# A planned kernel on one core: the same units in another written order, with other cells, other banks and 45 fill matmuls for 33

## The chip, the cores and the metric

The kernel runs on one core of one Trainium2 chip. The metric is device time in microseconds (us) of one execution. Three runs of the kernel before gave 459.48, 458.48 and 455.35 us, a median of 458.48 us.

## The reference

Inputs are float32: queries, keys and values of 4 batches, 8 heads, 768 positions and 40 channels, and three gates. Three blocks follow each other.

1. A recurrent attention over the 768 positions: a running maximum of the gates gives a forget and an input factor per position; a 40x40 state `C` and a vector `n` are updated with them, and each position reads `o * (C q) / max(|n q|, 1)`.
2. A gated convolution on the 320 joined channels: `(sigmoid(causal 5-tap conv of x) * (x @ w_val)) @ w_out`.
3. A mixer: the real part of a two-dimensional FFT over positions and channels is added to `x` (this is `u`), `u` is normalised, and `u + max(un @ w_ch1, 0) @ w_ch2` with 1280 hidden channels is returned.

## The kernel before

Per batch the 768 positions are six chunks of 128. A chunk (`a_fb` to `a_tr`) spreads the gates with a small matmul, scans them on VectorE into decays `d`, forms scores, state updates and outputs with many small matmuls on quarters of the array, divides, and transposes. After three chunks a half batch goes through the convolution (`p_conv`: 1 activation and 4 multiply-adds on VectorE per 128 channels; for three of the pieces five matmuls), the two products (`p_val`, `p_z`) and a fold; after six, the FFT as cosine and sine matmuls (`b_s`, `b_d`), the normalisation (`b_ln`), transposes (`b_ut`) and the feed-forward block (`m_1`, `m_2`) in three row blocks of five slices.

Matrix operands are split in two float32r parts, so that a product is three or four passes. The weights come as 64-bit words and are turned into float32 on the chip: `to_f32` takes two VectorE instructions that read two SBUF operands (`mk<-raw,mk`) and two that read one (`mk<-mk`) for each piece of 640 columns, and GpSimd forms the low parts. All of this conversion stands in batch 0.

**The order is written out.** The functions only record; each call becomes a unit (one VectorE, ScalarE, GpSimd or DMA instruction, or one group of matmuls), numbered as recorded. `emit` goes through `ORDER` and issues the units; each engine runs its own units in that order, and semaphores for true dependences come from the framework. `CELL` gives each working tile its SBUF slot or its first PSUM bank, which decides whose readers it must wait for. `FILLS` puts extra matmuls of ones on ones ahead of a unit, into a bank that is given as the third number; the second is how many. All DMAs but one are issued by SyncE (SP).

Units that the text names (batch, then chunk or block, in brackets):

| unit | engine | what |
|---|---|---|
| 11, 12, 13 | SP | loads of the forget gates `gf`, the input gates `gi`, the identity `pat` |
| 150 | SP | load of 64 rows of `w_val`, 160 KB |
| 25 | PE | first transposes of `gi` |
| 24, 26, 70 | DVE | scan to `eg`, copy to `isT`, first scan to `d` |
| 152, 153 | DVE | `mk<-mk` of a weight tail |
| 68, 78 | PE | gate spread of chunks (0,0) and (0,1) |
| 267 | PE | `a_pv` (0,3): reads `cc` and `e1`, then scores, then `d` |
| 266, 285, 288 | DVE | last `cc` of (0,3); scan to `d` of (0,5); product into `e1` for (0,5) |
| 416, 232 | PE | `a_pv` (0,5); the second `val` group (0,0,1) |
| 490, 516 | PE | the one-row matmul of `b_d` (0,0); first transposes of normalised rows |
| 690 | PE | scores and state products of chunk (1,0) |
| 514, 515, 576 | DVE, DVE, PE | low parts of the transposed rows (0,0); the first feed-forward group that reads them |
| 581, 583, 579, 580, 695 | PE, DVE, PE, PE, PE | `m_1` (0,0,1), its `hl`, the two halves of `m_2` (0,0,0), `a_pv` (1,0) |
| 788, 789, 813 | PE, DVE, PE | `val` (1,0,2), the product that reads it, `a_pv` (1,3) |

Of the kernel before, what the change touches and what calls it, by code (L numbers as in the profile page):

```python
# [176 lines left out]
]  # L177
FILLS = [
    (25, 15, 1), (72, 4, 1), (87, 2, 6), (485, 4, 6), (489, 3, 6), (516, 2, 6), (576, 3, 6),
]  # L180


# [1062 lines left out]
```

## Time and profile before

| | before |
|---|---|
| median of three runs | 458.48 us (455.35 to 459.48) |
| profiled execution, its own time | 456.86 us |
| span of that execution | 454.7 us |
| TensorE (PE) matmul busy | 436.1 us, 96% |
| VectorE (DVE) busy | 334.5 us, 74% |
| ScalarE (ACT) busy | 174.4 us, 38% |
| GpSimd (POOL) busy | 161.6 us, 36% |
| mean granted TensorE clock | 0.992 |

All rows are of the one profiled execution; its time outside the span is 2.2 us. Almost all instructions carry the line of the loop in `emit` (L304; L360 are fills and L367 is the warm-up), so the rows are read by tile names: `bank<-xH,wvH` is a matmul of a `val` group, `hl` the low part of a hidden slice. PE is the matmul row, PEld the weight loads, SPq the queue of DMA issues. Matmul ends are modelled, so starts are the safer reading.

### The profile page before, as it was taken

The page shows a single profiled execution, that of the slowest core. Times are in us where ns is not written, and L with a number is a line of the kernel's source. Part 1 is how long each engine was busy: PE and PEld are TensorE (multiplying, and loading weights), DVE is VectorE, ACT ScalarE, POOL GpSimd, SP SyncE. Part 2 cuts the span into 40 slices and gives each one's busy share as a digit, 9 for nine tenths or more (in the row PEclk, how much of TensorE's full clock was granted, in tenths as well). Part 3 has the DMA queues.
Part 4 walks back from the last instruction along what each step waited for, and adds up shares of the span by engine and source line. Part 5 has one row for each costly group of instructions (what it writes and reads, how often), then busy time and mean ns, then how long its engine had stood idle before and what let it go on. Part 6 is the DMA issues. An engine that isn't in the chain of part 4 may idle for free. (4 is left out here: it accounts for less than half of the span.)

```text
span 454.7 us, 13773 instructions
## 1 busy us (share of the span) xinstructions
PE 436.1 (96%) x5734; PEld 410.5 (90%) x5734; DVE 334.5 (74%) x810; ACT 174.4 (38%) x412; POOL 161.6 (36%) x210
## 2 busy tenths in 40 slices
PE   9978898799999999999999999999999999999996
PEld 8866777598999999999999999999999998999996
DVE  7999799989998886596686967788766846642421
ACT  4544644363343633232442524214425323160310
POOL 5666147577664513043524114544031130010000
PEclk9999899989999999999999999999999999999999
DMA  7779757661144511020303410213020000000011
GB/s 207 224 209 257 208 178 248 184 195 32 60 126 141 158 55 64 2 78 29 112 16 94 141 45 0 68 39 88 4 88 1 2 0 16 16 1 0 16 45 58
DMA packets 23301, 39.83 MB, mean 88 GB/s; under 512 B 4753, under 2 KB 14289, under 8 KB 23241
## 3 DMA queue, kind: packets, MB, share of 16 engines
q1 hardware_dynamic: 23192, 38.90, 28.7%
q8 instruction: 45, 0.74, 0.7%
q14 instruction: 16, 0.12, 0.1%
q0 software_dynamic: 48, 0.07, 0.1%
HBM read 32.77 MB, written 4.23 MB: 81 GB/s over the span
## 5 line engine op out<-in xcount | busy, mean ns | idle before, releaser
L304 PE MATMUL bank<-uu,w1H 128*128 128x256 f32 x480 | 92.5, 285 | 0.7 <-DVE uu L304 0.6
L304 PEld LDWEIGHTS bank<-uu,w1H 128*128 128x128 f32 x480 | 74.4, 188 | 2.9 <-issue 1.6
L304 PE MATMUL bank<-w2H,hh 128*128 128x320 f32 x240 | 75.9, 324 | 0.1
L304 PE MATMUL bank<-w2L,hh 128*128 128x320 f32 x240 | 72.4, 309 | 0.0
L304 PE MATMUL bank<-uu,w1L 128*128 128x256 f32 x240 | 67.3, 280 | 0.0
L304 ACT ACTIVATE hh<-bank 128x512 fp32r<-128x512 f32 x60 | 34.9, 594 | 69.7 <-PE bank L304 61.0
L304 DVE SCALAR_TENSOR_TENSOR hl<-bank,hh 128x512 fp32r<-128x512 f32 x60 | 40.4, 683 | 21.5 <-ACT hh L304 21.2
L304 PE MATMUL bank<-w2H,hl 128*128 128x320 f32 x240 | 54.9, 310 | 0.0
L304 DVE SCALAR_TENSOR_TENSOR bank<-xT,cw,bank 128x384 f32<-128x384 f32 x84 | 50.0, 617 | 2.1 <-ACT bank L304 1.3
L304 PEld LDWEIGHTS bank<-w2H,hh 128*128 128x128 f32 x240 | 45.1, 188 | 0.9 <-ACT dg L304 0.4
L304 PEld LDWEIGHTS bank<-w2L,hh 128*128 128x128 f32 x240 | 45.2, 188 | 0.2
L304 PEld LDWEIGHTS bank<-uu,w1L 128*128 128x128 f32 x240 | 45.3, 189 | 0.0
L304 PEld LDWEIGHTS bank<-w2H,hl 128*128 128x128 f32 x240 | 40.2, 188 | 0.0
L304 POOL TENSOR_TENSOR cc<-cc,fcol 128x164 f32<-128x164 f32 x40 | 19.9, 498 | 52.6 <-DVE cc L304 32.8
L304 DVE TENSOR_TENSOR z<-z,bank 128x320 f32<-128x320 f32 (+2 forms) x76 | 26.4, 375 | 16.3 <-PE bank L304 15.0
L304 POOL TENSOR_TENSOR gL<-gg,gH 128x384 fp32r<-128x384 f32 x16 | 18.5, 1158 | 54.1 <-ACT gH L304 40.4
L304 PE MATMUL bank<-uu,w1U 128*128 128x256 f32 x120 | 33.7, 281 | 0.0
L304 PE MATMUL bank<-uu,w1T 128*128 128x256 f32 x120 | 33.7, 281 | 0.0
L304 POOL TENSOR_TENSOR kvo<-kvo,r 128x320 f32<-128x320 f32 x24 | 17.8, 743 | 39.8 <-DVE r L304 32.7
L304 DVE TENSOR_TENSOR_SCAN d<-bank,pat 128x512 f32<-128x512 f32 x24 | 29.0, 1214 | 2.6 <-PE bank L304 2.4
L304 DVE SCALAR_TENSOR_TENSOR mk<-raw,mk 128x640 int32<-128x640 int32 (+2 forms) x30 | 27.2, 918 | 0.1
L304 POOL TENSOR_TENSOR e<-e,qk 128x512 f32<-128x512 f32 (+1 forms) x18 | 22.9, 1273 | 9.9 <-DMA qk<-in_qk_dram 5.4
(153 smaller groups left out, 998.8 us busy)
## 6 DMA issues: line engine op xcount, KB each, us to landing
kvo<-in_kvo_dram SPq DMA_DIRECT2D x24, 484.0 KB
qk<-in_qk_dram SPq DMA_DIRECT2D x48, 160.0 KB
raw<-in_w_dram SPq DMA_DIRECT2D x9, 640.0 KB
out_dram<-z SPq DMA_DIRECT2D x24, 160.0 KB
e<-sce SPq DMA_DIRECT2D x30, 80.0 KB
cs<-in_c_cs_dram SPq DMA_DIRECT2D x2, 386.0 KB
raw<-in_w_dram SPq DMA_DIRECT2D x4, 160.0 KB
raw<-in_w_val_dram SPq DMA_DIRECT2D x1, 640.0 KB
```

The lines of the kernel that those rows point to most:

```text
L304: i = getattr(engine, method)(*a, **k)
```

## The change

`ORDER`, `CELL` and `FILLS` are replaced; nothing else is. The units are the same 1996 and none is added. By engine, of 375 matmul groups 231 keep their place in PE's own order within two places (the farthest moves 25), of 809 VectorE units 343 do (44), of 410 ScalarE units 182 (184), of 206 GpSimd units 149 (34), of 196 DMA issues 79 (28). It comes from a search whose judgement of an order also counts stretches in which TensorE is little busy.

The diff, cut to the lines that the text speaks of (each `ORDER` line is whole):

```diff
 ORDER = [
-    11, 6, 12, 7, 16, 4, 0, 1, 13, 149, 150, 2, 15, 17, 9, 18, 22, 23, 32, 19, 21, 20, 14, 316, 33, 34, 115, 151,
-    114, 5, 315, 35, 25, 152, 139, 26, 24, 68, 153, 70, 8, 29, 116, 59, 117, 56, 72, 36, 30, 58, 154, 39, 140, 57,
...
-    280, 214, 47, 137, 127, 215, 283, 260, 287, 144, 158, 258, 217, 189, 266, 170, 216, 364, 159, 267, 145, 269,
-    285, 191, 218, 307, 220, 226, 136, 291, 171, 219, 270, 268, 236, 256, 161, 221, 271, 261, 272, 227, 288, 290,
...
-    713, 510, 523, 694, 516, 512, 525, 363, 397, 517, 518, 680, 735, 684, 513, 355, 681, 519, 1115, 708, 515, 514,
-    576, 526, 528, 577, 686, 685, 406, 530, 798, 687, 529, 531, 678, 719, 549, 710, 391, 578, 392, 826, 393, 532,
-    398, 581, 582, 583, 715, 533, 394, 808, 579, 580, 695, 534, 720, 712, 407, 600, 585, 535, 709, 697, 395, 696,
...
+    2, 7, 4, 11, 6, 150, 12, 13, 8, 3, 16, 15, 139, 1, 0, 17, 9, 22, 18, 114, 5, 32, 117, 23, 19, 115, 14, 25, 21,
+    20, 33, 37, 149, 58, 57, 116, 34, 28, 24, 68, 35, 78, 26, 70, 36, 151, 59, 56, 140, 39, 29, 27, 72, 38, 196,
+    118, 85, 77, 315, 30, 316, 76, 152, 75, 62, 80, 69, 153, 73, 107, 119, 154, 31, 71, 86, 317, 109, 318, 155, 87,
...
+    191, 126, 265, 260, 162, 266, 307, 283, 326, 258, 287, 291, 215, 267, 136, 285, 323, 288, 216, 217, 226, 144,
...
+    479, 361, 453, 376, 492, 493, 462, 682, 494, 681, 380, 49, 397, 495, 500, 490, 496, 520, 497, 387, 499, 347,
...
+    691, 510, 516, 527, 339, 517, 685, 355, 363, 694, 523, 512, 526, 519, 684, 518, 513, 713, 514, 515, 576, 525,
+    374, 718, 406, 1269, 528, 677, 719, 379, 735, 686, 577, 709, 530, 581, 531, 578, 582, 529, 391, 532, 687, 580,
+    714, 392, 533, 583, 695, 715, 393, 711, 585, 697, 534, 535, 1115, 549, 394, 550, 698, 398, 1279, 600, 536, 399,
...
+    820, 784, 827, 762, 596, 563, 592, 761, 631, 785, 786, 808, 625, 787, 597, 776, 626, 564, 788, 837, 804, 807,
+    789, 813, 763, 1111, 777, 829, 565, 815, 567, 838, 816, 817, 839, 840, 830, 566, 790, 764, 818, 814, 768, 778,
...
 ]
...
 FILLS = [
-    (25, 15, 1), (72, 4, 1), (87, 2, 6), (485, 4, 6), (489, 3, 6), (516, 2, 6), (576, 3, 6),
+    (25, 17, 1), (107, 4, 6), (181, 5, 6), (255, 2, 6), (295, 3, 6), (485, 3, 6), (489, 3, 6), (490, 3, 6),
+    (516, 3, 6), (576, 2, 6),
 ]
```

All 892 entries of `CELL` are written anew in the same way (slots, banks and accumulators).

## Rows read from the trace of the kernel before

**Rows 1.** The page: span, and busy time by engine.

```profile
span 454.7 us, 13773 instructions
PE 436.1 (96%) x5734; PEld 410.5 (90%) x5734; DVE 334.5 (74%) x810; ACT 174.4 (38%) x412; POOL 161.6 (36%) x210
```

**Rows 2.** The chain that ended last (start, duration, what): its long piece.

```profile
393.44 57.47 PE bank L304 x438
```

**Rows 3.** Busy time by stretch: start:end, length, then engines with instructions, clock, DMA.

```profile
0.00:96.42 96.42, 83.99 (x1296) 71.82 (x1296) 87.15 (x193) 48.38 (x117) 53.65 (x67) 0.96 0.74 214
49.65:53.06 3.41, 3.41 (x13) 3.31 (x14) 1.49 (x5) 2.19 (x6) 1.13 (x1) 0.50 0.66 149
90.61:94.02 3.41, 3.40 (x37) 3.28 (x38) 3.20 (x14) 2.97 (x7) 1.88 (x3) 0.50 0.98 270
96.42:135.00 38.58, 37.73 (x606) 35.78 (x607) 37.27 (x83) 16.61 (x35) 26.79 (x30) 1.00 0.27 85
135.00:450.90 315.90, 314.40 (x3835) 302.89 (x3834) 209.60 (x535) 109.36 (x260) 81.19 (x114) 1.00 0.16 50
```

**Rows 4.** Waits of VectorE from 0 to 96.42 us: total, times, longest.

```profile
DVE gg L304 <- PE bank L304: 1.9, 1, 1.9
DVE uu L304 <- ACT uu L304: 1.3, 1, 1.3
...
DVE isT L304 <- PE bank L304: 0.7, 1, 0.7
...
DVE mx L304 <- DMA gi<-in_ig_dram: 0.3, 1, 0.3
```

**Rows 5.** Timeline of PE and SP at the start: fills, first gate spread, a DMA issue.

```profile
5.83 3.51 PE L360 MATMUL bank<-ones 128*128 128x128 f32 x30
...
9.52 1.15 PE L304 MATMUL bank<-f,pat 128*64 128x64 f32 x32
...
2.69 0.59 SPq L304 DMA_DIRECT2D raw<-in_w_out_dram  x1
```

**Rows 6.** Timeline of VectorE at the start (brackets: idle before, and releaser).

```profile
10.33 0.29 DVE L304 TENSOR_SCALAR mk<-mk 128x320 int32<-128x320 int32 x1
10.71 1.22 DVE L304 TENSOR_TENSOR_SCAN d<-bank,pat 128x512 f32<-128x512 f32 x1
```

**Rows 7.** Timeline of PE around the first half-clock stretch, two `val` groups, with the multiply behind.

```profile
46.35 0.34 PE L304 MATMUL bank<-xH,wvT 128*128 128x384 f32 x1
46.53 0.34 PE L304 MATMUL bank<-xH,wvU 128*128 128x384 f32 x1
...
48.54 0.31 PE L304 MATMUL bank<-cc,e 40*64 40x41 f32 x4 [1.08 <-issue]
...
52.16 0.52 PE L304 MATMUL bank<-xH,wvT 128*128 128x384 f32 x1
52.48 0.52 PE L304 MATMUL bank<-xH,wvU 128*128 128x384 f32 x1
```

**Rows 8.** Timeline of PE ahead of the second half-clock stretch.

```profile
90.62 0.33 PE L304 MATMUL bank<-kvo 64*40 64x41 f32 x5 [1.72 <-DVE mv L304]
```

**Rows 9.** Timeline of PE: the matmuls of unit 267 that read `e1`.

```profile
36.07 0.68 PE L304 MATMUL bank<-cc,e 40*64 40x41 f32 x32
```

**Rows 10.** Groups by tile and form: shapes, count, busy us, mean ns, idle before.

```profile
L304 ACT ACTIVATE hh<-bank 128x512 fp32r<-128x512 f32 x60 | 34.9, 594 | 69.7 <-PE bank L304 61.0
L304 DVE SCALAR_TENSOR_TENSOR hl<-bank,hh 128x512 fp32r<-128x512 f32 x60 | 40.4, 683 | 21.5 <-ACT hh L304 21.2
```

**Rows 11.** Conversions on VectorE to 96.4 us: min/median/max ns, starts; then busy us, mean ns.

```profile
L304 DVE SCALAR_TENSOR_TENSOR mk<-raw,mk x24: 471/816/2195, 12.0 to 86.6; 128x640 int32<-128x640 int32 x16, 128x320 int32<-128x320 int32 x6, 128x15 int32<-128x15 int32 x2
...
L304 DVE SCALAR_TENSOR_TENSOR mk<-raw,mk 128x640 int32<-128x640 int32 x16 | 16.6, 1056 | 0.1
```

**Rows 12.** Timeline of VectorE and GpSimd beside each other.

```profile
80.40 1.53 POOL L304 TENSOR_TENSOR w1L<-mk,w1H 128x640 fp32r<-128x640 f32 x1
80.42 2.19 DVE L304 SCALAR_TENSOR_TENSOR mk<-raw,mk 128x640 int32<-128x640 int32 x1
```

243 rows, old and new, of tables (CELL, ORDER) are left out of this document.

## The prediction

> **What bounds the kernel now.** I read the page first: TensorE is busy for 96% of the span and no other engine comes near [rows 1]. Then the chain that ended last: its last long piece is 57.47 us of PE alone, 438 matmuls with no stall between them [rows 2]. Read by themselves, these say that only PE's work counts. The table by stretches says otherwise for the beginning [rows 3]. I cut it at 96.42 us, where the first feed-forward group (576) starts. Up to there VectorE is busy for 87.15 of 96.42 us and PE for 83.99: VectorE is the fuller of the two, and PE idles 12.43 us. From there to 135 us both are full (PE 37.73, VectorE 37.27 of 38.58), and from 135 to 450.9 PE idles 1.5 of 315.9 us. So the time is the moment at which 576 can start, plus 354.5 us of PE work with 0.85 + 1.5 = 2.35 us of idle time in it. What an order can win lies before 96.42 us: VectorE's own idle time, 96.42 - 87.15 = 9.27 us, and whatever makes its instructions longer. The waits of VectorE there say what it idled for [rows 4]: 1.9 us for a `val` group of PE, 1.3 us for ScalarE, 0.7 us for the first transposes, 0.3 us for a load.
>
> The granted clock is 0.50, the lower level of 1.2 GHz, in two stretches of 3.41 us [rows 3]. The longest of VectorE's waits ends in such a stretch. In the last two matmuls of a `val` group the starts are 0.18 us apart at full clock and 0.32 us at half [rows 7].
>
> **The change, part by part.** The sum is made against the profiled execution, 456.86 us: a span of 454.7 and 2.2 outside it. This is 1.6 us under the median of 458.48.
>
> *The work ahead of 576.* I counted the units that stand before it in both lists. On PE they are the same 63 groups. On VectorE, up to the later of 514 and 515, they are 193 in both lists, as in [rows 3], 192 of them shared; one addition into `z` (0.27 us) has changed places with its twin (0.24 us). After 576 the rest is therefore the same too. The new order can't take work from the stretch that VectorE bounds: 0.0 us.
>
> *The fills.* 33 before, 45 after. Fifteen took 3.51 us, so one is 0.234 us [rows 5], and twelve more are 2.8 us of PE time, all ahead of or at 576. They fall into PE's 12.43 us of idle time, so I take 0 for them, but for the first place, below. If that cover is gone, because VectorE arrives earlier, they cost up to +2.8.
>
> *The start.* The load of `gi` is now issued behind a weight load (150), which costs one issue more, 0.59 us [rows 5], and VectorE was already waiting 0.3 us for `gi` [rows 4]. The two extra fills hold the transposes (25) back by 2 x 0.234 = 0.47 us, and with them the gate spread (68), which takes 1.15 us [rows 5] and releases VectorE's first scan to `d`, 10.71 us before. Two narrow conversions (152, 153), 0.29 us the second [rows 6], no longer stand ahead of that scan but behind it. So VectorE is up to 0.47 + 0.6 = 1.1 us behind there. Later waits for data may absorb it: 0 to +1.1, and I take +0.5.
>
> *The clock.* The first half-clock stretch follows a chunk's small matmuls with a gap of 1.08 us [rows 7] and holds a `val` group of eight: 8 x (0.32 - 0.175) = 1.2 us, of VectorE's wait of 1.9. The second begins with the end of the gap of 1.72 us in the state products of chunk (1,0) (690) [rows 8]; VectorE is busy 3.20 of its 3.41 us [rows 3], so little hangs on it, and I take 0.5. The new order has three more fills ahead of 490 and one more ahead of 516, on both sides of 690, where PE waited before; ahead of 416 it has the three before 295. I take both stretches as gone: -1.7. The bounds are 0 (both stay) and -3.4 (in each, 3.41 us of work at half clock that would take 1.7, all of it on the path).
>
> *A new wait on VectorE.* Unit 288, the product into `e1`, stood ten VectorE units behind the scan 285 and now stands directly behind it. `e1` is read by the first matmuls of 267, which wait for the last `cc` (266). Between 266 and 288 VectorE now has only the scan, 1.22 us for that form [rows 6]; the matmuls that read `e1` last 0.68 us [rows 9]. If the wait is for those alone, it is nothing; if for all three parts of 267, taken as equally long, it is 3 x 0.68 - 1.22 = 0.8 us, and 1.0 with the hand-over. I take +0.3. Queued behind are two conversions and the rest of the chunk.
>
> *After 576.* Unit 695 must wait for `hl` of the slice before it (583). There were two halves of `m_2` between 581 and 695, now there is one: six matmuls at the pace of the last dense piece, 57.47 / 438 = 0.131 us [rows 2], 0.8 us. `hh` takes 0.59 and `hl` 0.68 us [rows 10], 1.27 together, and with the hand-overs, taken as 0.4, PE can be 0.9 us short. In the same way 813 now stands directly behind 788, with the product 789 to be awaited, and the output of chunk (1,4) behind a transpose: at the same price 0 to +2.7 together. But PE idles only 0.85 us in that stretch now [rows 3], and VectorE is full beside it, so that much of such a wait is one that would come anyway: +0.5. In return PE's 1.5 us of idle time behind 135 us [rows 3] can shrink: -0.5, of at most -1.5.
>
> *The DMA queue.* 117 of 196 issues moved by more than two places. VectorE waits for a transfer once, 0.3 us [rows 4], and the loads of chunk (0,0) stay ten issues deep. I take 0, and up to +1 where a weight piece comes late.
>
> Sum: 0 + 0 + 0.5 - 1.7 + 0.3 + 0.5 - 0.5 = -0.9 us; 456.86 - 0.9 = 456.0 us.
>
> **The rivals.** *VectorE's waits close (faster).* Its three largest waits of [rows 4], 1.9 + 1.3 + 0.7 = 3.9, are for PE or ScalarE results a few instructions away, and another order can put something between. With them gone and 1 us of the second stretch, 456.86 - 4.9 = 452.0. For it: the PE order is nearly kept, so what is freed is not paid for elsewhere. Against it: the start is worse, and in the same chains the new order has pairs about as close.
>
> *Conversions beside GpSimd (slower).* A conversion with two SBUF inputs took 2.19 us beside GpSimd's forming of a low part, itself 1.53 us long [rows 12], against a median of 0.816 us [rows 11]. The sixteen wide ones before 576 have a mean of 1.056 us [rows 11], so 16 x 0.24 = 3.8 us of VectorE's 87.15 are such lengthening already. Most of GpSimd's units and of these conversions have moved against each other. Each wide conversion that newly falls beside a low part costs 1.38 us of the engine that bounds the stage; five would make +6.9, 463.8, and from five on it decides. The same would work the other way if the 3.8 us came free. The Trainium skill (GPSIMD Engine Reference, Key points) states that GpSimd shares its SBUF interfaces with VectorE and contends with its instructions of two SBUF inputs; by that rule the chance is the same for all sixteen wherever GpSimd is busy, 53.65 of 96.42 us, and an order that does not look at it would come out about as long as this one. Here the rows agree on the lengthening; no row says how it falls in the new order.
>
> *The clock falls all the same.* The gap before the first stretch has no fill of its own. Then the sum is +0.8, 457.7: the change does not do what it is judged by, and nothing can be told from no change.
>
> **How the numbers follow.** A measurement of this kernel tells about 1% from no change: 4.6 us, so 453.9 and 463.1. The forecast has 0.37 and the rival with the clock 0.18, both within 1%. The rival with VectorE's waits has 0.32, and slower by the conversions, 0.13. The predicted time is that of the forecast, 456.0. The range reaches down to 450, 2 us under the rival's 452.0, and up to 462: the forecast with the upper bounds of the start, the new wait and the three waits after 576 (0.6 + 0.7 + 2.2), with the clock not won (1.7), is 461.2. The forecast's own range is 453 to 459. Faster by over 1%: 0.32; within: 0.55; slower: 0.13.
>
> **What would show it.** 576 starts within 2 us of 96.42 us, after the same 193 instructions of VectorE and the same 63 groups. The first scan to `d` starts later than 10.71 us. No stretch at clock 0.50 lies ahead of 576, and the wait for the `val` group is gone. 695 and 813 wait for VectorE. From 135 us on PE idles as little as now. It is wrong if VectorE's busy time before 576 moves by over 3 us from 87.15 (the conversions), if its idle time there falls under 5 us, or if a stretch at half clock appears behind 135 us.

## The result, and the profile after

The changed kernel took a median of 453.09 us (451.92 to 457.71, 20 executions) against 457.8 us of the kernel before (455.35 to 461.26, 20 executions): a ratio of 0.990, 95% interval 0.9876 to 0.9923. In a second series on another occasion it was 452.0 against 456.93, 0.9887 (0.986 to 0.9914). I had forecast 456.0, inside the 1% that counts as no change, with a range of 450 to 462. The time lies in the range, at the edge of that 1%, and 2.9 us under the forecast. The ratios, here and below, leave out executions that took over 1.5% longer than the fastest of their kernel (five of run 3, one each of runs 4, 8 and 10).

The profiled execution took 455.05 us, 2 us over the median, so it understates the change. The page of the changed kernel, span and busy time by engine (before: [rows 1]):

```profile
span 453.1 us, 13800 instructions
PE 435.7 (96%) x5758; PEld 411.4 (91%) x5758; DVE 327.0 (72%) x810; ACT 175.0 (39%) x412; POOL 158.5 (35%) x210
```

The instructions of VectorE are the same 810, yet it is busy for 7.5 us less; 5.7 of these lie behind 135 us, where PE is the full engine. The same kernel by stretches, cut at the start of 576 and at 135 us, and the one half-clock stretch ahead of the end (columns as in [rows 3]):

```profile
0.00:95.81 95.81, 84.39 (x1319) 72.64 (x1320) 86.19 (x195) 50.16 (x121) 49.90 (x66) 0.98 0.76 219
95.81:135.00 39.19, 38.90 (x618) 37.70 (x619) 36.41 (x85) 16.40 (x36) 27.72 (x32) 1.00 0.32 95
135.00:449.64 314.64, 312.43 (x3823) 301.10 (x3821) 203.94 (x531) 108.43 (x257) 80.90 (x113) 1.00 0.16 47
...
51.81:55.22 3.41, 3.41 (x13) 3.41 (x12) 2.06 (x7) 2.52 (x6) 0.92 (x2) 0.50 0.43 105
```

576 starts 0.61 us earlier, and in the second row PE idles 0.29 us where it idled 0.85. The first half-clock stretch of before is still there, over the same `val` group; the second is gone. The waits of VectorE ahead of 576 (before: [rows 4]):

```profile
DVE mx L305 <- DMA gi<-in_ig_dram: 1.4, 1, 1.4
DVE r L305 <- ACT r L305: 1.3, 2, 1.1
DVE gg L305 <- PE bank L305: 1.0, 1, 1.0
...
DVE uu L305 <- ACT uu L305: 0.2, 1, 0.2
```

The wait for `gi` grew by 1.1 us, where one issue had been priced at 0.6; the one for the `val` group halved, that for `uu` fell from 1.3 to 0.2. VectorE's idle time ahead of 576 as a whole did not fall in this execution: it is 95.81 - 86.19 = 9.62 us, for 9.27 before. The sixteen wide conversions ahead of 576, with busy time and mean (before: [rows 11], 16.6 us and 1056 ns), are the row that I had not counted on:

```profile
L305 DVE SCALAR_TENSOR_TENSOR mk<-raw,mk 128x640 int32<-128x640 int32 x16 | 14.9, 937 | 0.0
```

Since one execution is 1 to 2 us from another, a second profile of each kernel was taken (runs 5 and 11 below). The stretch ahead of 576 in these second profiles, first of before, then of the changed kernel:

```profile
0.00:96.13 96.13, 83.99 (x1296) 71.12 (x1296) 86.55 (x193) 48.12 (x117) 52.74 (x66) 0.96 0.71 214
...
0.00:94.62 94.62, 85.03 (x1320) 72.81 (x1320) 87.18 (x195) 50.06 (x121) 49.75 (x66) 0.98 0.73 222
```

This table is worked out from the timelines of all four. Records of VectorE overlap a little, so their durations sum to more than the engine was busy; the row below the sum counts overlaps once.

| us | before, two profiles | changed, two profiles |
|---|---|---|
| start of unit 25 | 9.28, 8.94 | 9.13, 9.71 |
| 25 to 576 | 87.14, 87.19 | 86.68, 84.91 |
| durations of the same 193 VectorE instructions ahead of 576, summed | 99.2, 98.3 | 96.9, 98.0 |
| the same 193, overlaps counted once | 87.5, 86.9 | 85.9, 86.9 |
| VectorE's idle time ahead of 576 | 9.27, 9.58 | 9.62, 7.44 |
| of the 193, sixteen wide conversions, summed | 16.89, 16.89 | 14.99, 14.67 |
| 576 to 841 | 48.67, 48.69 | 47.84, 47.78 |
| 841 to the last matmul | 305.80, 305.92 | 305.98, 304.92 |
| last VectorE instruction to the end of the span | 3.25, 3.25 | 2.93, 2.94 |

The wide conversions differ the same way in both pairs. The idle time does not, and in the second profile of the changed kernel VectorE is as busy as before and waits less. One group (572, three transposes, some 0.3 us) stands ahead of 841 in the new order and behind it in the old one, so the stretch from 576 to 841 gained that much more on equal work, and the one behind it that much less.

Each execution's granted clock is recorded too. Call lost clock (1 - clock) x span. Over 88 executions of the kernel before, beside the experiments, the mean is 457.1 us at a clock of 0.992 (3.7 us lost), and a straight line through them gives 455.1 us at full clock and 0.53 us more for each us lost. Over 26 of the changed kernel it is 453.1 us at 0.998 (0.8 lost), 452.6 at full clock. Of 3.9 us between the means, about 1.5 go with the clock and 2.5 with the order.

### The profile page after: what moved, and what is told of

It reads as the page before. It is cut to its first block, busy times and chain, and to the rows that moved or that the text cites. A ratio compares the mean times of both kernels' runs of the same rounds, so it can differ in the third digit from the quotient of the medians.

```text
span 453.1 us, 13800 instructions
## 1 busy us (share of the span) xinstructions
PE 435.7 (96%) x5758; PEld 411.4 (91%) x5758; DVE 327.0 (72%) x810; ACT 175.0 (39%) x412; POOL 158.5 (35%) x210
## 4 chain that ended last, share of the span: by engine, by line
PE 75%; DVE 15%; issue 3%; ACT 2%; POOL 2%; DMA 2%; SPq 0%; DVEq 0%; ACTq 0%; POOLq 0%
PE bank L305 74%; DVE mk L305 5%; DVE d L305 2%; DVE z L305 1%; DMA qk<-in_qk_dram 1%; POOL kvo L305 1%; DVE bank L305 1%; PE bank L368 1%; PE bank L361 1%; DVE bs L305 1%; DVE uu L305 1%; DVE hl L305 1%; DMA woU<-tl 1%; DVE gg L305 1%; DVE cc L305 1%
## 5 line engine op out<-in xcount | busy, mean ns | idle before, releaser
L305 POOL TENSOR_TENSOR cc<-cc,fcol 128x164 f32<-128x164 f32 x40 | 18.9, 473 | 71.6 <-DVE cc L305 49.6
L305 DVE TENSOR_TENSOR z<-z,bank 128x161 f32<-128x161 f32 (+2 forms) x76 | 27.1, 374 | 20.0 <-PE bank L305 18.4
L305 POOL TENSOR_TENSOR gL<-gg,gH 128x384 fp32r<-128x384 f32 x16 | 17.4, 1092 | 46.7 <-ACT gH L305 41.7
L305 POOL TENSOR_TENSOR e<-e,qk 128x512 f32<-128x512 f32 (+1 forms) x18 | 21.9, 1214 | 9.0 <-DMA qk<-in_qk_dram 3.7
L305 ACT ACTIVATE r<-bank 128x8 f32<-128x8 f32 x24 | 4.3, 178 | 50.9 <-PE bank L305 43.8
```

Of the source, the lines that this page charges most:

```text
L305: i = getattr(engine, method)(*a, **k)
```

## The experiments

OLD and NEW are the two lists of the diff ahead; cells and fills go with the order unless said. Ratios are to the kernel before, on the same chip.

**Runs 1, 2 and 7: where the gain lies.** Run 1, `e1_new_front`:

```diff
-ORDER = OLD
+ORDER = NEW[:526] + [n for n in OLD if n not in NEW[:526]]   # up to 576
```

> The new order, cells and fills up to and including unit 576, the old order behind it (cells renamed so that the tiles alive at the cut keep theirs; one bank chosen anew). Theory A (the gain lies ahead of 576: the second half-clock stretch is gone, VectorE's instructions there are 2.2 us shorter): 453 to 454 us, nearly all of the change. Theory B (the gain lies behind 576, in shorter waits there, and the front gives only the 0.6 us by which 576 started earlier in the one profiled execution): 457.2 us. In both, 576 starts as in the changed kernel, near 95.8 us.

455.81 us, 0.9976 (0.995 to 1.0001). Neither theory: 576 starts 85.0 us behind 25, as early as in the changed kernel's second profile, but then the old order gives 0.8 us back. Its timeline of PE, the first matmuls of unit 695:

```profile
102.17 0.69 PE L311 MATMUL bank<-qk 40*64 40x64 f32 x32 [1.31 <-DVE d L311]
```

PE arrived earlier at a VectorE that is full, and waited. 576 to 841 took 49.46 us, for 48.7 with the old front and 47.8 with the new order. The front alone is worth little without the order behind it.

Run 2, `e2_old_front`, the complement (one reader of a bank, 715, moved ahead of 695, so that the bank is free):

```diff
-ORDER = NEW
+ORDER = OLD[:528] + [n for n in NEW if n not in OLD[:528]]   # up to 576
```

> The complement: the old order, cells and fills up to and including 576, the new order behind it. Theory A: 457 to 458 us, no change from before, 576 near 96.4 us and two stretches at half clock. Theory B: 453.7 us. If both halves give part, this one and the other kernel's gains add up to 4.7 us.

461.65 us, 1.0094 (1.0061 to 1.0127): both theories missed. The mean clock of its seven executions is 0.984. The profiled one, in the view by stretches, has ten microseconds at half clock in the front, and a second stretch at 223.9 us:

```profile
22.52:32.76 10.24, 10.08 (x184) 8.85 (x184) 7.78 (x22) 3.49 (x10) 4.63 (x8) 0.50 0.53 161
```

Up to 576 this kernel is the kernel before, unit for unit, so the length of the first stretch is not the edit's. Behind 576 it is slower: 50.40 us to 841, for 48.7 (0.3 of the difference is group 572). So the two halves do not add up. Run 7, `e7_new_to_850`, moves the cut back:

```diff
-ORDER = NEW
+ORDER = NEW[:816] + [n for n in OLD if n not in NEW[:816]]   # up to 850
```

> The new order, cells and fills up to and including unit 850 (two thirds of the units are still to come, all of batch 0 and the attention of batch 1 lie ahead), the old order behind it. With the cut at 576 the kernel took 455.8. If the rest of the gain lies between 576 and 850, where VectorE is still full: 453.1, as the changed kernel. If it lies behind 850, where TensorE has nothing to wait for: 455.5 us.

454.84 us, 0.9951 (0.9927 to 0.9974), between the two expectations. 576 to 841 takes 47.80 us, as in the changed kernel; behind 841 it has 305.55 us and the old 3.24 us at the end. Of the whole gain a part comes only with the new order behind 850: at full clock run 7 takes 454.2 us and the changed kernel 452.6. The gain is spread over all three parts. The last is the least certain in size: behind 841 the changed kernel's own two profiles differ by 1 us.

**Runs 3, 6, 4 and 12: fills and clock.** Run 3, `e3_new_order_old_fills`, the new order with the old fills:

```diff
-    (25, 17, 1), (107, 4, 6), (181, 5, 6), (255, 2, 6), (295, 3, 6), (485, 3, 6), (489, 3, 6), (490, 3, 6),
-    (516, 3, 6), (576, 2, 6),
+    (25, 15, 1), (72, 4, 1), (87, 2, 6), (485, 4, 6), (489, 3, 6), (516, 2, 6), (576, 3, 6),
```

> The new order and cells with the 33 old fills at their old units. If the twelve more fills took the second half-clock stretch away, it comes back: PE clock 0.50 for 3.4 us ahead of 576, mean clock 0.992, about +1 us, 454.1. If the order alone did it, 453.1 and clock 0.996 to 1.0 as now. If the fills stood in the way of TensorE, a gain: under 452.5.

Median 458.37 us of twelve, from 451.94 (clock 0.996) to 462.08 (0.981), mean clock 0.987. The ratio of 0.9978 (0.9942 to 1.0015) is that of the seven shortest, which have a mean of 456.1 us at 0.990. The line through the twelve gives 452.2 us at full clock, with 0.97 us for each us lost; it reaches far, for 5.9 us were lost on average. The fills did not take a stretch or two away: without them the new order loses more clock than the old one. The profiled execution, PE ahead of the fall, and the view by stretches:

```profile
22.97 0.43 PE L310 MATMUL bank<-pat,gi 32*128 32x32 f32 x4
23.81 0.31 PE L310 MATMUL bank<-cc,e 40*64 40x41 f32 x2 [0.42 <-DVE cc L310]
25.94 0.35 PE L310 MATMUL bank<-cc,e 40*64 40x41 f32 x4 [1.82 <-DVE cc L310]
```
```profile
23.81:25.40 1.59, 0.31 (x2) 0.19 (x2) 0.63 (x3) 0.95 (x4) 1.45 (x3) 1.00 0.98 261
25.40:32.23 6.83, 6.17 (x138) 5.82 (x138) 4.45 (x15) 1.77 (x5) 2.98 (x6) 0.50 0.30 93
```

PE waits for `cc` twice, and the clock falls to half for 6.83 us. Run 6, `e6_new_order_fill_181`, adds one site:

```diff
-    (25, 15, 1), (72, 4, 1), (87, 2, 6), (485, 4, 6), (489, 3, 6), (516, 2, 6), (576, 3, 6),
+    (25, 15, 1), (72, 4, 1), (87, 2, 6), (181, 5, 6), (485, 4, 6), (489, 3, 6), (516, 2, 6), (576, 3, 6),
```

> The new order and cells with the 33 old fills and one new site, five fills ahead of unit 181, the small matmuls at 23.7 us, where the kernel with the old fills alone fell to half clock at 25.4 us. If that site is what holds the clock in the new order: mean clock 0.995 or more and 452.5 to 453.5 us. If all new sites are needed: clock 0.987 to 0.99 and 456 to 458 us, as with the old fills.

453.4 us, 0.9913 (0.9888 to 0.9939), mean clock 0.996 (452.4 us at full clock): with five matmuls more at this one site most of the clock and of the time is back; the changed kernel beside it had 452.0 and 0.999. The same place on PE:

```profile
22.81 0.43 PE L310 MATMUL bank<-pat,gi 32*128 32x32 f32 x4
23.17 1.38 PE L366 MATMUL bank<-ones 128*128 128x128 f32 x10
24.48 0.31 PE L310 MATMUL bank<-cc,e 40*64 40x41 f32 x2
25.75 0.44 PE L310 MATMUL bank<-cc,e 40*64 40x41 f32 x16 [0.96 <-DVE cc L310]
```

They fill 1.38 us in which PE would wait, and `cc` is read hardly later: 17.02 us behind unit 25, for 16.84.

Run 4, `e4_old_order_new_fills`, the old order with the new fills:

```diff
-    (25, 15, 1), (72, 4, 1), (87, 2, 6), (485, 4, 6), (489, 3, 6), (516, 2, 6), (576, 3, 6),
+    (25, 17, 1), (107, 4, 6), (181, 5, 6), (255, 2, 6), (295, 3, 6), (485, 3, 6), (489, 3, 6), (490, 3, 6),
+    (516, 3, 6), (576, 2, 6),
```

> The old order and cells with the 45 new fills. If the fills carry the gain through the clock: both half-clock stretches or the second one are gone, 455 to 456.5 us. If the order carries it: 457.8 us or a little more (12 fills are 2.8 us of PE time, hidden in idle time at best), clock 0.992.

457.82 us, 0.9993 (0.9971 to 1.0015), clock 0.995, 456.4 at full clock: what the clock gave was lost again. Its wide conversions take 16.82 us and its 576 to 841 is 48.71, as before. Its 25 to 576 is 87.27 us, with the changed kernel's fills and 3.41 us at half clock like the changed kernel's profiles: at equal fills and clock the new order is some 1.7 us shorter there (one profile against the mean of six). Fill sites belong to an order. Run 12, `e12_two_more_sites`:

```diff
...
+    (416, 3, 6), (673, 5, 6),
...
```

> The new order and fills with two more sites, three fills ahead of 416 and five ahead of 673, where the profiles of the new order still fell to half clock (51.8, and 75.8 to 77.6 us). If those are the places where it is still lost: mean clock 0.999 to 1.0 in all executions, and a smaller spread, 452 us (at the slope of 0.5 us per us of lost clock, the 0.9 us lost now are worth 0.45). If the fills delay TensorE where VectorE waits for it: 453 to 454.

453.99 us, 0.9934 (0.9908 to 0.9959), clock 0.999. The mean clock came as expected and the time did not: at full clock 453.9, 1.3 us over the changed kernel. In the profiled execution the clock was at half from 28.12 to 31.53 us, which neither new site covers. The last lost clock costs more to buy than it is worth, and no run beat the changed kernel.

**Run 8, the start.** `e8_start_undone`:

```diff
-    2, 7, 4, 11, 6, 150, 12, 13, 8, 3,
+    2, 7, 4, 11, 6, 12, 13, 150, 8, 3,
...
-    (25, 17, 1),
+    (25, 15, 1),
```

> The new order with the start of before: the weight load 150 behind the gate loads 12 and 13 again, and 15 fills ahead of unit 25 for 17. If the start costs what I took (+0.5 us, at most 1.1): 452.6 us, with the first scan to d 0.5 to 1 us earlier. If the wait for the gates is absorbed by later waits: 453.1, no change.

452.72 us, 0.9917 (0.9889 to 0.9944), between 452.0 and 453.1 of the changed kernel's two series: a cost of the start is not told from nothing, and half a microsecond isn't ruled out. The wait for `gi` fell to 0.5 us, and the first scan to `d`, at 10.44 us, then waited 0.67 us for PE. In thirteen of fourteen profiles this scan follows unit 25 by 1.43 to 1.47 us, whatever the order. Unit 25 stands behind TensorE's warm-up and the first fills, at 8.73 to 10.55 us; the clock rose at 4.0 to 7.0 us, with no relation to the order.

**Runs 5 and 11, second profiles.** `e5_changed_again` and `e11_before_again` have no edit.

> The changed kernel as it is, for more executions beside the others on one chip and a second profile. The one profiled execution (455.05 us) stands 2 us above the median. If that was the start (TensorE's clock rises at another time in each execution) and one half-clock stretch, then here about 453 us with 576 at 94 to 95 us and mean clock 0.998. If the first runs were favoured by the chip, 455 us.

452.0 us, clock 0.999. In its profile (452.78 us), 576 starts at 94.62 us; the only half-clock stretch ahead of the end lies at 76.92, not at 51.81.

> The kernel before as it is, for a second profile: if its stages repeat, the wide conversions take 16.8 to 16.9 us again, 576 starts 87 us behind unit 25 and 841 starts 48.7 us behind 576. The half-clock stretches may lie elsewhere.

456.43 us, 1.0008 (0.9971 to 1.0044). The stages repeat to 0.12 us and the wide conversions to 0.01, but not the clock: the stretch lies at 31.87 to 38.70, where the first profile had two of 3.41 us at 49.65 and 90.61. The lengthened conversions are the same ones. VectorE, then GpSimd, of this second profile of before:

```profile
79.44 0.81 DVE L310 SCALAR_TENSOR_TENSOR mk<-raw,mk 128x640 int32<-128x640 int32 x1
80.82 2.20 DVE L310 SCALAR_TENSOR_TENSOR mk<-raw,mk 128x640 int32<-128x640 int32 x1
84.97 2.14 DVE L310 SCALAR_TENSOR_TENSOR mk<-raw,mk 128x640 int32<-128x640 int32 x1
87.04 1.35 DVE L310 SCALAR_TENSOR_TENSOR mk<-raw,mk 128x640 int32<-128x640 int32 x1
...
80.80 1.54 POOL L310 TENSOR_TENSOR w1L<-mk,w1H 128x640 fp32r<-128x640 f32 x1
84.90 1.54 POOL L310 TENSOR_TENSOR w1L<-mk,w1H 128x640 fp32r<-128x640 f32 x1 [2.56 <-ACT w1H L310]
86.39 1.32 POOL L310 TENSOR_TENSOR kvo<-kvo,isT 128x328 f32<-128x328 f32 x1
87.67 1.31 POOL L310 TENSOR_TENSOR kvo<-kvo,d 128x320 f32<-128x320 f32 x1
```

Four of the sixteen are longer than 0.85 us: these three and one of 1.39 us beside `tl` at 72 us. The same stretch of the changed kernel:

```profile
81.64 1.51 DVE L305 SCALAR_TENSOR_TENSOR mk<-raw,mk 128x640 int32<-128x640 int32 x1
83.72 1.51 DVE L305 SCALAR_TENSOR_TENSOR mk<-raw,mk 128x640 int32<-128x640 int32 x1
85.81 0.81 DVE L305 SCALAR_TENSOR_TENSOR mk<-raw,mk 128x640 int32<-128x640 int32 x1
86.61 0.81 DVE L305 SCALAR_TENSOR_TENSOR mk<-raw,mk 128x640 int32<-128x640 int32 x1
...
78.72 1.05 POOL L305 TENSOR_TENSOR kvo<-kvo,d 128x320 f32<-128x320 f32 x1
79.73 0.98 POOL L305 TENSOR_TENSOR kvo<-kvo,isT 128x328 f32<-128x328 f32 x1
80.68 3.87 POOL L305 TENSOR_TENSOR w1L<-mk,w1H 128x640 fp32r<-128x640 f32 x2
```

GpSimd's two products into `kvo` now stand ahead of the conversions, and the low parts meet them for part of their time. Over 0.81 us, the old order pays 0.58 + 1.39 + 1.33 + 0.54 = 3.8 us, the new one 0.58 + 0.70 + 0.70 = 2.0.

In the other conversions that GpSimd meets, it is GpSimd that takes longer. In this second profile of before the conversion at 59.34 us took 0.83 us beside `gL`, the one at 79.44 us 0.81 beside `e`:

```profile
58.80 2.23 POOL L310 TENSOR_TENSOR gL<-gg,gH 128x384 fp32r<-128x384 f32 x1 [5.06 <-ACT gH L310]
...
78.65 2.19 POOL L310 TENSOR_TENSOR e<-e,qk 128x256 f32<-128x256 f32 x1
```

Without such a neighbour `gL` took 1.02 us and `e` 0.75. In every overlap of over 0.2 us in the two profiles shown here, one of the two is lengthened: either the conversion, which then ends 0.68 us behind GpSimd's instruction, or GpSimd's instruction, which outlasts the conversion.

**Runs 9 and 10: is that on the path?** ScalarE writes the weights' low parts, as one rounded copy; the subtraction of the high part is left out:

```diff
-            WLO.tensor_tensor(l, x, f(h), op=ALU.subtract)
+            A.activation(l, x, AF.Copy)
```

Run 9, `e9_old_low_on_act`, in the old order:

> The old order, cells and fills, with the weights' low parts written by ScalarE instead of GpSimd, as one rounded copy of the weight (the subtraction of the high part is left out). Theory C (the conversions on VectorE are longer beside GpSimd's low parts, and that sets the start of 576): the sixteen wide conversions with two SBUF inputs fall from 16.9 us to about 13.1 (16 x 0.82), 576 starts 2 to 4 us earlier against unit 25, and the time is 453 to 455 us. Theory D (their length is hidden by waits): the conversions shorten, 576 and the time stay, 457 us. If ScalarE, which gets the work, becomes what VectorE waits for: later than 457.

453.58 us, 0.9932 (0.9902 to 0.9961), at a clock of 0.994. The wide conversions take 13.8 us, 3.1 less, and 576 starts 84.03 us behind 25, 3.1 us earlier: theory C. The stretch ahead of 576 in this run:

```profile
0.00:93.37 93.37, 81.68 (x1295) 69.84 (x1296) 82.74 (x194) 53.31 (x127) 41.97 (x58) 0.99 0.73 222
```

VectorE is busy for 4 us less, since other instructions were shorter too, and idles 10.6 us, about 1 more. Run 10, `e10_new_low_on_act`, in the new order:

> The same edit on the new order, cells and fills (the subtraction is left out here too). In the new order the wide conversions take 14.5 to 15.0 us instead of 16.9. Theory C: they fall to about 13.1, less than with the old order, and the gain is half as large: 1 to 2 us, 450.5 to 451.5. Theory D: 452 to 453. If GpSimd's low parts were not what lengthens them, they stay at 14.5 or more.

Its wide conversions, and its wait of VectorE for `uu`, both ahead of 576:

```profile
L311 DVE SCALAR_TENSOR_TENSOR mk<-raw,mk 128x640 int32<-128x640 int32 x16 | 12.9, 814 | 0.0
```
```profile
DVE uu L311 <- ACT uu L311: 1.5, 2, 0.9
```

454.54 us, 0.9952 (0.9921 to 0.9982), not faster but some 1.5 to 2.5 us slower than the changed kernel. No wide conversion ahead of 576 is lengthened any more, but 576 comes 85.3 us behind 25, no earlier. VectorE now waits 1.5 us for ScalarE's `uu`, 0.2 in the changed kernel; its whole idle time there, 94.92 - 85.73 = 9.2 us, is within that of the changed kernel's two profiles, so what held 576 back is not shown. So the low parts do lengthen the conversions, in both orders. In the old order 576 came earlier by as much as the wide conversions lost, 3.1 us; in the new one 1.8 us more brought nothing. GpSimd was relieved, with all its work, and ScalarE loaded by the same edit, so what the new order's 1.9 to 2.2 us of shorter conversions are worth by themselves is argued from these runs and not measured.

## Why the prediction was right or wrong

**The place** was right: up to 576, VectorE; the 193 instructions and 63 groups stand ahead of it in both. But 576 is not where VectorE's hold ends. Run 1 shows that PE waits at 695 for what it gained at 576.

**The work ahead of 576, 0.0 us: this step failed.** The instructions are the same, their durations are not: over six profiles of the new front with the new fills they sum to 96.4 to 98.0 (mean 97.1), over two of before and run 4 to 98.3 to 99.4 (mean 99.0), 1.9 us more. With overlaps counted once it is 86.1 against 87.5, 1.4 us, and single profiles scatter by as much. The wide conversions alone are 2.1 us shorter, the two of 15 columns 0.9, while some other instructions are longer. The rival on conversions had the mechanism and the price of 1.38 us beside a low part [rows 12], but asked only how many might newly fall there, when four of sixteen did already. It said that the 3.8 us could come free as well and gave that no chance. About half came free. By the rule of the Trainium skill (GPSIMD Engine Reference, Key points), which I read as an equal chance wherever GpSimd is busy, the new order would be about as long. Runs 9 and 10 agree that VectorE's instructions with two SBUF inputs are lengthened beside GpSimd; but ahead of 576 it was always the same three or four, beside `w1L`, `tl` and `kvo`, and beside `gL` and `e` GpSimd paid. That is not a draw: each order has its own sum, 16.8 to 16.9 us in four profiles of the old front, 14.5 to 15.0 in eight of the new.

**The rival with VectorE's waits** gave the time, 452.0, and not the way to it. The waits for the `val` group and for `uu` shrank, others grew: VectorE's idle time ahead of 576 was 9.3 and 9.6 us before and 8.7 on average in the six profiles (7.4 to 9.6). The forecast's own net ahead of 576 (start, clock and 288), -0.9, is near that -0.8 by luck, for its single terms came out otherwise.

**The fills, 0.** Their own time is not seen in the new order (452.6 us at full clock with 45, 452.4 with the 38 of run 6); in the old order the new ones cost about 1.3 us at full clock (run 4), and eight more in the new order about as much (run 12).

**The clock, -1.7:** the size was right, about -1.5, by luck, for the reasoning was not. I took two places for what happens in every execution. They move: 49.65 and 90.61 us in one profile of before, 31.87 in the other, 51.81 and 76.92 in the changed kernel's. That is why the stretch at 51.81, which I had as gone, is there in the first profile, and why a mean over executions, not a profile, shows the change. The one site that was tried by itself, ahead of 181, did most of the work and covers a place that had no fall in the one profile I had.

**The start, +0.5:** the wait for `gi` came, and nothing of it is found in the time (run 8). The first scan to `d`, forecast later than 10.71 us, came at 10.56 and 11.14.

**The wait on VectorE at 288, +0.3:** none. The scan 285 ends at 38.49 us and 288 starts at 38.41, overlapping it.

**After 576, +0.5:** measured -0.85 us, the same to 0.06 us in six profiles with the new order up to 841 (runs 10 and 12: -0.5 and -0.4). 695 starts 4.9 us behind 576 in them and waits 0.15 us for `hl`, not 0.9, since its first matmuls don't wait for it:

```profile
101.99 0.50 PE L305 MATMUL bank<-kvo 64*40 64x41 f32 x30 [0.15 <-DVE hl L305]
```

No wait of 0.15 us or more stands at 813. I priced the pairs that moved together and left out those that moved apart: PE's idle time from 576 to 841 fell from 0.85 to 0.28 us, and VectorE's conversions there, six, from 5.92 to 5.09.

**Late, -0.5:** over five profiles of the new order (the two of the table, and 305.58, 303.93 and 305.25 of runs 6, 8 and 12; run 3's 309.86 holds 6.83 us at half clock) -0.7 on average, within the bound of -1.5. Some 0.3 of this is group 572, which only moved ahead of 841. The term's reason, less idle time of PE, is not seen: behind 135 us PE idled 1.5 and 1.8 us before, and 2.2, 1.4, 2.0, 0.6 and 1.5 in the five. Where the rest comes from stays open. The 0.3 us at the end, behind the last addition, I had not looked at.

In sum: 25 to 576 about -1.6 us over six profiles, then -0.85, -0.7 and -0.3, some 3.5 us, of the 3.9 between the means. Part of the first may be clock, for the profiles of before spent 6.83 us at half clock there and these 3.41. The rest up to 3.9 may be clock that these profiles, at 0.995 to 0.996, lost and the average execution, at 0.998, did not. Of the signs that I had named, VectorE's busy time ahead of 576 moved by under 1 us and its idle time stayed over 5, so bounds of 3 and 5 us were too wide to notice what changed.

Open: why runs 2 and 3 also fell to half clock at 220 to 224 us, far behind the last fill; and what decides whether the conversion or GpSimd's instruction pays for an overlap, since `e` began 0.79 us ahead of its conversion and still was the longer one (VectorE's `mk<-mk` had begun at 78.64 us, just ahead of it).

## What to carry to other kernels

When an order changes and the instructions do not, price their durations too: list the instances of each form on the engine that bounds the stage, see which are longer than the shortest, and look up in both orders what GpSimd does beside those few, and how long that took. A half-clock stretch in one profile is one draw, so take the clock over many executions and look for every gap in small matmuls where it could fall. A fill is free only where the engine waits anyway, and such places must be found anew for each order.

## What the runs showed of the hardware

TensorE fell to its lower level of 1.2 GHz at other places in each execution of one kernel, and a microsecond of lost clock cost about half a microsecond of time (0.53 over 88 executions of the kernel before; 0.97 over the twelve of run 3). In run 3 the fall came after 0.31 us of matmuls in 1.59 us. The first rise of the clock, at 4.0 to 7.0 us, went with a start of unit 25 that differs by up to 1.4 us with the same fills (9.13 and 10.55 us). A conversion of 128x640 with two SBUF inputs took 0.81 us by itself and 0.93 to 2.20 us where it waited for a GpSimd instruction beside it; in the other overlaps GpSimd's took longer, 2.23 us for 1.02 with `gL`.
